# A gated mix of linear and local attention on one core: evacuations first, later weight sums, zeros between weight chunks, and KV products on 128x32 tiles

## The chip, the cores and the metric

The kernel runs on one core of a Trainium2 chip. The metric is the device time of one execution in microseconds (us). Before the change three runs took 472.9, 471.93 and 472.41 us; the median is 472.41 us. The engines are named as in the profile: PE is TensorE's matmul, PEld its weight load, DVE is VectorE, ACT is ScalarE, POOL is GpSimd, and SP is the engine whose queue issues nearly all the DMAs (SPq in the profile).

## The reference

Two attention blocks read the same input x (2048 rows of 1024), each with weights of its own, and a gate mixes their outputs:

```python
x = A_x
g = sigmoid((x * gate_w).sum(-1, keepdims=True))
return g * a + (1 - g) * b
```

Block A is linear attention with 32 heads of 32 columns, without a causal mask:

```python
phi = lambda t: jnp.where(t > 0, t + 1, jnp.exp(t)) + 1e-6
pq, pk = phi(q), phi(k)
kv = jnp.einsum("bhsd,bhse->bhde", pk, v)
z = jnp.einsum("bhsd->bhd", pk)
num = jnp.einsum("bhqd,bhde->bhqe", pq, kv)
den = jnp.einsum("bhqd,bhd->bhq", pq, z)[..., None] + 1e-6
a = (num / den) merged over heads @ wo
```

So for each head the kernel needs one 32x32 matrix kv and one column z, both sums over all 2048 rows. Block B is a softmax over the 8 positions s, s-2, ... s-14 of each row, for 32 heads, followed by its own output product `@ wo`. All inputs are bf16.

## The kernel before

**Products.** Most projections are done as block products of two by two halves with seven multiplications in place of eight (m1 to m7, `class Group`, line 235 on). They need sums of halves of the operands, built on VectorE: of x (`xsums`), of the weights (`Weights.sums`, lines 133 to 136, four operations for a whole weight matrix), and of the attention outputs (`out_sums`, line 762). Each product ends in a PSUM tile X or Y of one bank, of which there are four in all; ScalarE copies X out (line 259) or VectorE adds X or Y to a saved part (line 232).

**Stages, in the order of time.** First `vb_plain` (line 459) computes the B values of four row tiles with ordinary products, while the weights arrive in chunks of two of the eight k blocks (`vb_load`). In its loop over kc the first tile has to wait for each chunk. Before it, TensorE multiplies zeros (line 810) that come from `KVacc`, which is cleared for it. The B values then go to DRAM (`vb_store`), and the loads of later x tiles stand behind these stores on SP's queue. From about 70 to 310 us follow in turn the B keys and queries by columns (`k_group`, `q_group`), the A keys and values by rows (`ka_group`, `va_group`), and beside them the side work. From about 300 us on come the A queries (`qa_plain`, line 597), from about 360 us on the output products (`out_group`).

**Side work.** `attn` (lines 632 to 682), the KV products (`kv` inside `va_group`) and the A outputs (`qa_out`) are generators. `add_side(delay, ...)` puts them into a queue, and `side` takes a step of one of them between the products of the main loop, at a rate and not before its delay, counted in products, is over. So the delay places the TensorE work of a step. All of them write into one and the same PSUM tile of four banks (`side_ps`, `ps_s` has a single buffer). A step can start only when the step before has been read out of it:

- scores `s` (line 647) are read by the exponential on ScalarE (line 652), which makes PT;
- `o` (lines 664 and 670) is read by Ln on ScalarE (line 675) and by the copy `nB` on VectorE (line 676);
- `kps` (line 529), the KV products of one pair of row tiles, is read by the addition to `KVacc` on VectorE (line 537; a copy at line 535 the first time). After the last of eight, line 539 masks KVacc into `KVz`, which the A outputs use;
- `oA` (line 568) is read by a copy on ScalarE (line 570). Then GpSimd computes line 573 and line 574, VectorE the reciprocal (line 576), and GpSimd two products (line 579); the result is stored to `OA_d` (line 581), and comes back transposed as `oT` (line 754) for the output products.

The KV products take 128 columns of phi(k) at a time, which are four heads, against the values of these four heads with a column of ones each (4 x 33 = 132 columns). Of the 4 x 4 head blocks of each result only the four on the diagonal are used; the mask `bd` clears the others.

**Order.** TensorE and SP follow the order in which the program calls them. For the other engines a scheduler places instructions by priority and expected readiness when the kernel is built; each of these engines then works through its list in order. `defer(products, ops, gap)` hands VectorE the sums of a weight matrix, one operation every `gap` products, after `products` products: the sums of A's output weights begin 15 products after the pair-7 keys, those of B's 7 products after `plain(1, 0)`.

**In qa_plain** each row half has two PSUM tiles Q (line 610). ScalarE takes the exponential of each (line 615); when both are there, VectorE does line 618 and twice line 620, which releases the two tiles.

Of the kernel before, what the change touches and what calls it, by code (L numbers as in the profile page):

```python
# [8 lines left out]
ACT = mybir.ActivationFunctionType  # L9
ALU = mybir.AluOpType  # L10
AX = mybir.AxisListType
BF16 = mybir.dt.bfloat16
FP16 = mybir.dt.float16
F32 = mybir.dt.float32
P = 128
QB = 57
NPAIR = 9
TW = 6 * QB
# [10 lines left out]
def kernel(  # L29
# [11 lines left out]
    nc = tc.nc  # L41
# [6 lines left out]
    SCALE = float(Dh) ** -0.5  # L48
# [9 lines left out]
    consts = ctx.enter_context(tc.tile_pool(name="consts", bufs=1))  # L58
# [109 lines left out]
        return Weights(P, W, T)  # L168


    KVacc = consts.tile([P, 8, 132], F32, name="KVacc")
    nc.vector.memset(KVacc[:, 0:1, :], 0.0)
    warm = KVacc.bitcast(BF16)[:, 0, 0:256]
    W = wp.tile([P, 8, D], BF16, name="W", tag="W")
    T = tp.tile([P, 3, 4, 512], FP16, name="T", tag="T")
    T3v = kqp.tile([P, 4, 512], FP16, name="T3v", tag="kq")
# [138 lines left out]
    def add_side(delay, gen, key, kind, front=False):  # L315

        entry = [state["now"] + delay, gen, key, next(gen)[1], kind]
        if front:
            queue.insert(0, entry)
        else:  # L320
            queue.append(entry)
# [39 lines left out]
    def defer(products, ops, gap=1):  # L361


        deferred.append([state["now"] + products, list(ops), gap])
# [50 lines left out]
    gps_tile = side_ps("gps")  # L415
# [9 lines left out]
    def gate_end():  # L425
# [2 lines left out]
        nc.vector.tensor_scalar(out=omg[:], in0=omg[:], scalar1=1.0, scalar2=None, op0=ALU.add)  # L428
        nc.vector.reciprocal(out=omg[:], in_=omg[:])


    def v_tiles(name):
        if name == "va":
# [26 lines left out]
    def vb_plain(*pairs):  # L460


        vs = {pair: v_tiles("va") for pair in pairs}
        tiles = [(pair, i) for pair in pairs for i in range(2)]

        def ps_of(pair, i):
            return ps_pj.tile([P, 512], F32, name="K", tag="XY"[i] + str(pair % 2))

        def mm(ps, pair, i, j, kc):
            p, c = divmod(pair, 4)  # L470
            nc.tensor.matmul(ps[:], lhsT=xT[p][:, kc, i, c * P:c * P + P],
                             rhs=wvB.W[:, kc, 512 * j:512 * j + 512], start=kc == 0, stop=kc == 7,
                             skip_group_check=True)
        for pair, i in tiles:
            ps = ps_of(pair, i)
            for kc in range(8):
                mm(ps, pair, i, 0, kc)
            gate(tile_of(pair, i))
            v_final(vs[pair], True)(i, 0, ps[:], None)
        tiles = tiles[2:] + tiles[:2]  # L480
        ps = {t: ps_of(*t) for t in tiles}
        for k in range(4):
            for t in tiles:
                for kc in (2 * k, 2 * k + 1):
                    mm(ps[t], *t, 1, kc)
                if k == 3:
                    pair, i = t
                    v_final(vs[pair], True)(i, 1, ps[t][:], None)
                    vb_store(vs[pair], pair, i)
# [27 lines left out]
    def va_group(w, pair):  # L517
        vs = v_tiles("vA")

        def kv():  # L520
            first = kv_state["n"] == 0
            kv_state["n"] += 1
            last = kv_state["n"] == 8
            yield 0, 3
            kps = side_ps("kps")
            for i in range(2):
                pk = pks[tile_of(pair, i)]
                for c in range(8):
                    nc.tensor.matmul(kps[:, c // 2, c % 2 * 132:c % 2 * 132 + 132], lhsT=pk[:, c * P:(c + 1) * P],  # L529
                                     rhs=vs[i][:, 4 * c:4 * c + 4, :].rearrange("p h e -> p (h e)"),  # L530
                                     start=i == 0 and c % 2 == 0, stop=i == 1, skip_group_check=True)
            src = kps[:, :, 0:264]
            dst = KVacc[:].rearrange("p (a c) e -> p a (c e)", a=4)
            if first:
                nc.vector.tensor_copy(out=dst, in_=src)
            else:
                nc.vector.tensor_tensor(out=dst, in0=src, in1=dst, op=ALU.add)
            if last:
                nc.vector.tensor_tensor(out=KVz[:].rearrange("p c (g e) -> p c g e", g=4),
                                        in0=KVacc[:].rearrange("p c (g e) -> p c g e", g=4),  # L540
                                        in1=bd[:, None, :, :].broadcast_to([P, 8, 4, 33]), op=ALU.mult)
            yield 2, 2

        def done(i):
            if i == 1:
                add_side(2, kv(), 2, "kv", True)
        return Group(row_ops(w, pair), v_final(vs), done)


# [84 lines left out]
    def attn(nn, p, kT, qT, vw):  # L634

        def scores(t):
            s = side_ps("s")
            for ch in range(2):  # L640
                for j in range(3):
                    e = (3 * ch + j) * QB
                    for b in range(2):
                        q0 = q_of(t, j, b)
                        k0 = max(0, q0 - 7)
                        for g in range(4):
                            nc.tensor.matmul(s[64 * b:64 * b + 64, g, e:e + QB],  # L647
                                             lhsT=kT[32 * g:32 * g + 32, 1024 * ch + k0:1024 * ch + k0 + 64],
                                             rhs=qT[32 * g:32 * g + 32, 1024 * ch + q0:1024 * ch + q0 + QB],
                                             start=True, stop=True)  # L650
            PT = ptp.tile([P, 4, TW], BF16, name="PT", tag="PT")
            nc.scalar.activation(out=PT[:], in_=s[:, :, 0:TW], func=ACT.Exp, scale=SCALE)  # L652
            m = maskp[:, 0 if t else 1, :, :].rearrange("p i q -> p (i q)")
            nc.vector.tensor_tensor(out=PT[:], in0=PT[:], in1=m[:, None, :].broadcast_to([P, 4, TW]), op=ALU.mult)  # L654
            return PT

        def pv(t, PT):
            o = side_ps("o")
            for e in range(6):
                ch, j = divmod(e, 3)  # L660
                for g in range(4):
                    for b in range(2):
                        rows = slice(64 * b, 64 * b + 64)
                        nc.tensor.matmul(o[32 * g:32 * g + 32, 2 * b, QB * e:QB * e + QB],
                                         lhsT=vw[rows, 3 * t + j, 4 * ch + g, :],
                                         rhs=PT[rows, g, QB * e:QB * e + QB], start=True, stop=True)
            for g in range(4):
                for b in range(2):
                    rows = slice(64 * b, 64 * b + 64)
                    nc.tensor.matmul(o[32 * g:32 * g + 32, 2 * b + 1, 0:TW], lhsT=ones[rows, :], rhs=PT[rows, g, :],  # L670
                                     start=True, stop=True)
            nB = ofp.tile([P, 2, TW], F32, name="nB", tag="nB", bufs=1)
            rB = ofp.tile([P, 2, TW], F32, name="rB", tag="rB", bufs=1)
            oB = ofp.tile([P, 6, 2, QB], BF16, name="oB", tag="oB", bufs=2)
            nc.scalar.activation(out=rB[:], in_=o[:, 1:4:2, 0:TW], func=ACT.Ln)  # L675
            nc.vector.tensor_copy(out=nB[:], in_=o[:, 0:4:2, 0:TW])  # L676
            nc.scalar.activation(out=rB[:], in_=rB[:], func=ACT.Exp, scale=-1.0)
            num, r = (ap.rearrange("p b (e q) -> p e b q", e=6) for ap in (nB[:], rB[:]))
            nc.vector.tensor_tensor(out=oB[:], in0=num, in1=r, op=ALU.mult)
            nc.sync.dma_start(out=OB_d[p][2 * nn:2 * nn + 2, :, TW * t:TW * t + TW].rearrange("c p q -> p c q"),  # L680
                              in_=oB[:].rearrange("p (c j) b q -> p c (j b q)", c=2))

        last = None
        yield 0, 2
        for t in range(4):
            if t < 3:
                PT = scores(t)
                yield (1, 3) if last else (3, 3)
            if last:
                pv(*last)  # L690
                yield 1, 3
            last = (t, PT)
# [29 lines left out]
    Wo = {}  # L722

    def load_wo(k, src):
        Wo[k] = row_weights(src, 0)
# [80 lines left out]
        return Group(operands, final, nk=8, scale=sc)  # L806


    for _ in range(20):
        nc.tensor.matmul(gps_tile[:, 1, 0:256], lhsT=warm[:, 0:P], rhs=warm, start=True, stop=True)  # L810

    wkB, wqB, wqA = {}, {}, {}

# [58 lines left out]
    rows = []  # L872
    for pair in range(1, 7):
        rows += [(ka[pair],), (va[pair - 1],)]
    rows += [(ka[7], lambda: load_wo("A", A_wo), lambda: defer(15, Wo["A"].sums(), 3)), (va[6],),
             (va[7], lambda: load_wo("B", B_wo))]
    cols = []
    for nn in (1, 2, 3):
# [27 lines left out]
    load_qa(2)()  # L906
    plain(0, 0, load_qa(3))
    plain(1, 0)
    defer(7, Wo["B"].sums(), 4)
    plain(2, 0)  # L910
    plain(3, 0)
    plain(0, 1, lambda: later(3, lambda: (drain(0), out_in(9, 0, 1, 2)())))
# [40 lines left out]
```

## Time and profile before

| | |
|---|---|
| three runs, median | 472.41 us (471.93 to 472.9) |
| the profiled execution | 472.19 us |
| its span, first to last instruction | 470.3 us |
| mean granted TensorE clock | 0.993 |
| matmuls of `kps` (line 529), 8 x 16 | 8.9 us busy, 220 ns each |
| addition to KVacc (line 537), 7 times | 1257 ns each |
| copy nB (line 676), 24 times | 20.8 us busy, 867 ns each |
| GpSimd's products obA (line 579) | 23.9 us busy, 1108 ns each |
| zeros at the start (line 810), 20 matmuls | 4.1 us busy, 394 ns each |

A busy time of TensorE counts each matmul from its start to its modelled end, and neighbours overlap: 16 KV matmuls of 220 ns take less than a microsecond together. So what a group of matmuls costs TensorE is best read from where the next group starts. In the lists in order of time the columns are the start, the length of the merged piece, the engine, the line, the operation with its tiles and shapes, the count, and in brackets the idle time of the engine before it with what ended it. In the list of waits they are who waited, for whom, the sum in us, the count, and the longest.

### The profile page before, as it was taken

Reading aid. Unit: us, or ns where it says so; the run is one execution under the profiler, and the core shown is the slowest. Engines: PE = TensorE matmul, PEld = TensorE weight load, DVE = VectorE, ACT = ScalarE, POOL = GpSimd, SP = SyncE. Lnnn points to the kernel's source line nnn. Section 1 sums busy time; section 2 is a strip of 40 time slices with the busy share of each in tenths; the row PEclk is TensorE's granted clock in tenths of the full one; section 3 lists DMA queues with packets and bytes.
Section 4 is the critical chain, followed back from the end, with each engine's and each line's share of the span. In section 5 each row is a group of like instructions: output and inputs, shape, how many; then the busy total and the mean of one; then the engine's idle time right before and its main releaser. Section 6 shows DMA issues by size and latency. Waiting matters only on the chain. (4 is left out here: it accounts for less than half of the span.)

```text
span 470.3 us, 11050 instructions
## 1 busy us (share of the span) xinstructions
PE 450.5 (96%) x4656; PEld 220.0 (47%) x4732; DVE 286.0 (61%) x458; ACT 230.3 (49%) x331; POOL 64.1 (14%) x145
## 2 busy tenths in 40 slices
PE   7989999999999999999999999999999999999997
PEld 3445444444444445444444444545545444444443
DVE  0436678669748677586674856597856772165311
ACT  1233337558568485584865847535564432222221
POOL 8000000000000000000000000006877631000000
PEclk8989999999999999999999999999999999999999
DMA  7999721491110602106122055436239981599111
GB/s 175 185 219 231 256 61 63 122 258 29 45 43 20 157 13 70 29 16 148 26 58 41 16 136 179 114 114 171 59 81 180 197 192 56 102 183 195 59 46 45
DMA packets 117650, 51.60 MB, mean 110 GB/s; under 512 B 77664, under 2 KB 115552, under 8 KB 117600
## 3 DMA queue, kind: packets, MB, share of 16 engines
q1 hardware_dynamic: 117504, 50.88, 46.2%
q8 instruction: 37, 0.61, 0.6%
q0 software_dynamic: 96, 0.01, 0.2%
q14 instruction: 13, 0.11, 0.1%
HBM read 25.69 MB, written 16.79 MB: 90 GB/s over the span
## 5 line engine op out<-in xcount | busy, mean ns | idle before, releaser
L610 PE MATMUL Q<-xT,WS 128*128 128x512 bf16 x246 | 57.3, 379 | 1.0 <-DVE eq L620 0.4
L250 PEld LDWEIGHTS <-xT 128*128 128x128 bf16 (+1 forms) x352 | 33.3, 98 | 39.7 <-issue 2.2
L250 PE MATMUL X<-T,SS 128*128 128x512 f16 x176 | 45.2, 379 | 0.0
L259 ACT COPY U4s<-X 128x512 f32<-128x512 f32 x38 | 22.1, 582 | 40.7 <-PE X L250 40.7
L652 ACT ACTIVATE PT<-s 128x1368 bf16<-128x1368 f32 x24 | 31.5, 1311 | 20.9 <-PE s L647 20.8
L250 PE MATMUL Y<-W,xT 128*128 128x512 bf16 (+1 forms) x137 | 38.0, 386 | 1.8 <-issue 1.1
L250 PEld LDWEIGHTS <-SS 128*128 128x128 f16 x264 | 24.6, 98 | 28.5 <-issue 1.1
L250 PEld LDWEIGHTS <-WS 128*128 128x128 bf16 (+1 forms) x256 | 24.0, 98 | 29.2 <-issue 2.0
L610 PEld LDWEIGHTS <-WS 128*128 128x128 bf16 x256 | 24.4, 98 | 27.5 <-issue 1.1
L615 ACT ACTIVATE eq<-Q 128x512 bf16<-128x512 f32 x32 | 19.1, 598 | 31.8 <-PE Q L610 30.7
L654 DVE TENSOR_TENSOR PT<-PT,maskp 128x1368 bf16<-128x1368 bf16 x24 | 20.8, 867 | 20.8 <-ACT PT L652 20.8
L250 PE MATMUL Y<-xT,WS 128*128 128x512 bf16 (+1 forms) x128 | 32.9, 380 | 0.0
L250 PE MATMUL X<-SS,TS 128*128 128x512 f16 x128 | 32.8, 379 | 0.0
L250 PEld LDWEIGHTS <-oT 128*128 128x128 bf16 (+1 forms) x192 | 18.8, 98 | 23.4 <-issue 0.6
L250 PEld LDWEIGHTS <-TS 128*128 128x128 f16 x192 | 18.0, 98 | 20.7 <-issue 1.1
L259 ACT COPY U2s<-X 128x512 f32<-128x512 f32 x38 | 22.1, 582 | 9.1 <-PE X L250 9.1
L676 DVE COPY nB<-o 128x684 f32<-128x684 f32 x24 | 20.8, 867 | 8.7 <-ACT rB L675 8.2
L259 ACT COPY M1s<-X 128x512 f32<-128x512 f32 x38 | 22.2, 583 | 7.8 <-PE X L250 7.7
L579 POOL TENSOR_TENSOR obA<-ofv,rec 128x512 bf16<-128x512 f32 x22 | 23.9, 1108 | 8.3 <-DVE rec L576 7.7
L250 PE MATMUL Y<-W,oT 128*128 128x512 bf16 (+1 forms) x96 | 22.7, 379 | 0.6 <-DVE osb L802 0.6
L250 PE MATMUL X<-W,SS 128*128 128x512 bf16 x80 | 22.8, 388 | 0.4
L250 PE MATMUL X<-T,oS 128*128 128x512 f16 x96 | 22.7, 379 | 0.0
(125 smaller groups left out, 742.2 us busy)
## 6 DMA issues: line engine op xcount, KB each, us to landing
OB_d<-oB SPq DMA_DIRECT2D x24, 171.0 KB, 3.0
V_d<-va SPq DMA_DIRECT2D x16, 256.0 KB, 2.7
WS<-in_B_wqkv_dram SPq DMA_DIRECT2D x16, 256.0 KB, 4.2
W<-in_A_wqkv_dram SPq DMA_DIRECT2D x8, 512.0 KB, 6.2
OA_d<-obA SPq DMA_DIRECT2D x16, 256.0 KB, 2.4
out_dram<-osb SPq DMA_DIRECT2D x32, 128.0 KB, 1.9
oT<-OB_d SPq DMA_DIRECT2D x12, 256.0 KB, 4.7
vw<-V_d SPq DMA_DIRECT2D x8, 288.0 KB, 4.8
```

What stands on the lines that cost most here:

```text
L250: nc.tensor.matmul(ps[:], lhsT=lhsT, rhs=rhs, start=start and kc == 0, stop=kc == self.nk - 1, skip_group_check=True)
L259: nc.scalar.copy(out=s[:], in_=ps[:])
L579: nc.gpsimd.tensor_tensor(out=ob[:, k:k + 2], in0=of[:, k:k + 2, :, 0:32], in1=rec[:, k:k + 2].broadcast_to([P, 2, 8, 32]), op=ALU.mult)
L610: nc.tensor.matmul(ps[:], lhsT=w.W[:, kc, j * P:j * P + P], rhs=xT[p][:, kc, i, :], start=kc == 0, stop=kc == 7, skip_group_check=True)
L615: nc.scalar.activation(out=es[i][:, j, :], in_=ps[:], func=ACT.Exp)
L652: nc.scalar.activation(out=PT[:], in_=s[:, :, 0:TW], func=ACT.Exp, scale=SCALE)
L654: nc.vector.tensor_tensor(out=PT[:], in0=PT[:], in1=m[:, None, :].broadcast_to([P, 4, TW]), op=ALU.mult)
L676: nc.vector.tensor_copy(out=nB[:], in_=o[:, 0:4:2, 0:TW])
```

## The change

There are four parts.

1. **Start.** The zero tile is now the whole KVacc in its new, smaller shape (264 fp32 numbers per partition, against 132 that were cleared before). 24 instead of 20 zero matmuls run first, and in the first tile of `vb_plain` three more run ahead of each of the kc = 2, 4 and 6, where the next weight chunk begins.
2. **KV products.** Each head's 32 columns of phi(k) are multiplied by its own 33 columns of values, on a tile of 128 rows by 32 columns of the array: 64 matmuls instead of 16 for a pair. The four heads of a group land in four bands of 32 partitions of the same 33 columns, all in one PSUM bank. KVacc shrinks from 1056 to 264 numbers per partition; the mask multiplies it, broadcast four times, into the same KVz.
3. **Priority.** The exponential that reads the scores, and Ln and the copy nB that read `o`, are placed by the scheduler at high priority.
4. **Delays.** The KV products come with a delay of 3 products instead of 2, and of 5 for the last pair. The sums of A's output weights are deferred by 24 products instead of 15, those of B's by 14 instead of 7.

```diff
-    KVacc = consts.tile([P, 8, 132], F32, name="KVacc")
-    nc.vector.memset(KVacc[:, 0:1, :], 0.0)
-    warm = KVacc.bitcast(BF16)[:, 0, 0:256]
+    KVacc = consts.tile([P, 8, 33], F32, name="KVacc")
+    nc.vector.memset(KVacc[:], 0.0)
+    warm = KVacc.bitcast(BF16)[:].rearrange("p a b -> p (a b)")[:, 0:256]
...
+    def warm_up(n):
+        for _ in range(n):
+            nc.tensor.matmul(gps_tile[:, 1, 0:256], lhsT=warm[:, 0:P], rhs=warm, start=True, stop=True)
+
...
             for kc in range(8):
+                if (pair, i) == tiles[0] and kc in (2, 4, 6):
+                    warm_up(3)
                 mm(ps, pair, i, 0, kc)
...
                 for c in range(8):
-                    nc.tensor.matmul(kps[:, c // 2, c % 2 * 132:c % 2 * 132 + 132], lhsT=pk[:, c * P:(c + 1) * P],
-                                     rhs=vs[i][:, 4 * c:4 * c + 4, :].rearrange("p h e -> p (h e)"),
-                                     start=i == 0 and c % 2 == 0, stop=i == 1, skip_group_check=True)
-            src = kps[:, :, 0:264]
-            dst = KVacc[:].rearrange("p (a c) e -> p a (c e)", a=4)
+                    for g in range(4):
+                        h = 4 * c + g
+                        nc.tensor.matmul(kps[32 * g:32 * g + 32, 0, 33 * c:33 * c + 33],
+                                         lhsT=pk[:, 32 * h:32 * h + 32], rhs=vs[i][:, h, :],
+                                         start=i == 0 and c == 0, stop=i == 1, skip_group_check=True)
+            acc_ = KVacc[:].rearrange("p c e -> p (c e)")
             if first:
-                nc.vector.tensor_copy(out=dst, in_=src)
+                nc.vector.tensor_copy(out=acc_, in_=kps[:, 0, 0:264])
             else:
-                nc.vector.tensor_tensor(out=dst, in0=src, in1=dst, op=ALU.add)
+                nc.vector.tensor_tensor(out=acc_, in0=kps[:, 0, 0:264], in1=acc_, op=ALU.add)
             if last:
                 nc.vector.tensor_tensor(out=KVz[:].rearrange("p c (g e) -> p c g e", g=4),
-                                        in0=KVacc[:].rearrange("p c (g e) -> p c g e", g=4),
+                                        in0=KVacc[:, :, None, :].broadcast_to([P, 8, 4, 33]),
                                         in1=bd[:, None, :, :].broadcast_to([P, 8, 4, 33]), op=ALU.mult)
...
-                add_side(2, kv(), 2, "kv", True)
+                add_side(5 if pair == 7 else 3, kv(), 2, "kv", True)
...
-            nc.scalar.activation(out=PT[:], in_=s[:, :, 0:TW], func=ACT.Exp, scale=SCALE)
+            with tc.high_priority():
+                nc.scalar.activation(out=PT[:], in_=s[:, :, 0:TW], func=ACT.Exp, scale=SCALE)
...
-            nc.scalar.activation(out=rB[:], in_=o[:, 1:4:2, 0:TW], func=ACT.Ln)
-            nc.vector.tensor_copy(out=nB[:], in_=o[:, 0:4:2, 0:TW])
+            with tc.high_priority():
+                nc.scalar.activation(out=rB[:], in_=o[:, 1:4:2, 0:TW], func=ACT.Ln)
+                nc.vector.tensor_copy(out=nB[:], in_=o[:, 0:4:2, 0:TW])
...
-    for _ in range(20):
-        nc.tensor.matmul(gps_tile[:, 1, 0:256], lhsT=warm[:, 0:P], rhs=warm, start=True, stop=True)
+    warm_up(24)
...
-    rows += [(ka[7], lambda: load_wo("A", A_wo), lambda: defer(15, Wo["A"].sums(), 3)), (va[6],),
+    rows += [(ka[7], lambda: load_wo("A", A_wo), lambda: defer(24, Wo["A"].sums(), 3)), (va[6],),
...
-    defer(7, Wo["B"].sums(), 4)
+    defer(14, Wo["B"].sums(), 4)
```

## Prediction, made before the changed kernel was run

> **What bounds the kernel now.** I read the page first (engine shares and slices), then the list of waits with TensorE as the one that waits, then the order of time of TensorE, VectorE and GpSimd around each of its stalls, and last the compiled instruction order of both kernels, engine by engine.
>
> ```profile
> PE 450.5 (96%) x4656; PEld 220.0 (47%) x4732; DVE 286.0 (61%) x458; ACT 230.3 (49%) x331; POOL 64.1 (14%) x145
> PE   7989999999999999999999999999999999999997
> PEclk8989999999999999999999999999999999999999
> ...
> PE s L647 <- DVE nB L676: 3.2, 7, 1.0
> PE K L471 <- DMA W<-in_B_wqkv_dram: 2.2, 1, 2.2
> ```
>
> TensorE is busy from end to end, so time is won only where it stands still, where its clock is halved, or where its work shrinks. The change touches four places.
>
> Place 1, the start (order of time of TensorE; then the table of windows, whose last four fields are POOL busy, clock, DMA share, GB/s):
>
> ```profile
> 1.04 4.06 PE L810 MATMUL gps<-KVacc 128*128 128x256 bf16 x20 [1.04 <-DVE KVacc L172]
> 7.30 3.41 PE L471 MATMUL K<-W,xT 128*128 128x512 bf16 x8 [2.19 <-DMA W<-in_B_wqkv_dram]
> ...
> 8.00:11.40 3.40, 3.40 (x16) 1.37 (x16) 0.00 (x0) 0.59 (x1) 2.86 (x15) 0.50 1.10 199
> 31.90:35.30 3.40, 3.40 (x10) 1.18 (x8) 0.80 (x2) 0.59 (x1) 0.00 (x0) 0.50 1.18 198
> ```
>
> After the zeros TensorE stands for 2.19 us, and then runs at half clock for one stretch of 3.4 us. A second such stretch follows the waits for xT at 29 to 31 us.
>
> Place 2, the attention stretch, 70 to 300 us (VectorE, then TensorE):
>
> ```profile
> 173.02 0.42 DVE L498 TENSOR_SCALAR tA<-tA 128x1024 bf16<-128x1024 bf16 x1
> 173.35 0.42 DVE L499 TENSOR_SCALAR eA<-eA 128x1024 bf16<-128x1024 bf16 x1
> 173.69 0.86 DVE L676 COPY nB<-o 128x684 f32<-128x684 f32 x1
> ...
> 174.60 0.56 PE L647 MATMUL s<-qT,kT 32*64 32x57 bf16 x48 [0.48 <-DVE nB L676]
> ```
>
> The next scores need the one side tile of PSUM (four banks) that nB still reads.
>
> Place 3, the last KV products (TensorE, then VectorE):
>
> ```profile
> 309.41 1.24 PE L529 MATMUL kps<-vA,eA 128*128 128x132 bf16 x16 [1.03 <-DVE nB L676]
> ...
> 307.36 1.22 DVE L133 TENSOR_TENSOR T<-W 128x2048 f16<-128x2048 bf16 x1
> 308.49 0.86 DVE L676 COPY nB<-o 128x684 f32<-128x684 f32 x1
> ```
>
> A Wo sum of 1.2 us sits ahead of nB, and the KV products wait for nB.
>
> Place 4, the plain q groups, 317 to 360 us (GpSimd, VectorE, TensorE):
>
> ```profile
> 339.58 1.17 POOL L573 TENSOR_SCALAR rec<-of 128x32 f32<-128x32 f32 x1
> 343.73 0.32 POOL L573 TENSOR_SCALAR rec<-ofv 128x32 f32<-128x32 f32 x1
> 350.28 0.32 POOL L573 TENSOR_SCALAR rec<-of 128x32 f32<-128x32 f32 x1
> ...
> 350.95 0.35 DVE L576 RECIPROCAL rec<-rec 128x32 f32<-128x32 f32 x1 [2.89 <-POOL rec L574]
> ...
> 352.36 2.75 PE L610 MATMUL Q<-xT,WS 128*128 128x512 bf16 x12 [0.35 <-DVE eq L620]
> ```
>
> GpSimd's units of L573, L574, L579 follow each other without a hole from 327 to 353 us: 3.3 us a unit, 4.2 us where a Wo sum on VectorE lies over it (L573 takes 1.17 instead of 0.32). Its ninth unit releases the reciprocal, behind which L618 and L620 stand in VectorE's queue, and TensorE waits for L620. So here GpSimd already sets the pace.
>
> [...] the trace shows the drain (about 0.09 us before each scores block, 0.13 after it)[...].
>
> **Part by part**, against the profiled execution (472.19 us with 470.3 of span, 0.22 under the median 472.41).
>
> A. KV products. Now 16 matmuls and 0.94 us a time (127.68 to 128.62), eight times. After: 64 pairs of load and matmul on 128x32 tiles, 33 columns. No row has this tile. The nearest, L664 (48 pairs on 64x32), runs a pair in 8.3 ns in its steady part, with some 0.1 us of stalled start inside; each row group then takes a load every 16.6 ns. At 8.3 ns: 64 x 8.3 = 0.53, plus drain 0.09, inner stall 0.09, tail 0.12, in all 0.83 us, a gain of 8 x 0.11 = 0.9. If a load that fills all rows goes only at the 16.6 ns of a row group: 1.06 + 0.30 = 1.36, a loss of 8 x 0.42 = 3.3. I take -0.9, since L647 and L664 show loads into neighbouring tiles overlapping; both ends are kept. [...] The products come one product later (five for pair 7); GpSimd's memset of the next vA waits for them, but is needed 15 us later.
>
> B. Priority. ScalarE's order is the same in both kernels. VectorE's differs at three of the third scores blocks (113, 173 and 233 us): nB passes one L499, 0.34 us. At 173 and 233 TensorE gains that, 0.68 in all: Ln ends at 173.21, so nB can start at 173.36. At 113 VectorE is full from 107 to 122 us, and vA at 119.27 would stop TensorE by as much more: 0. The other waits of about 0.35 us stay, since nB there follows Ln at once. L499 and L500 finish up to 0.9 us later; their KV product is over 10 us off. B = -0.7.
>
> C. Place 3. L133 now follows the third L620 pair, so nB runs at 307.4; the KV products come 12 Q matmuls later (2.6 us) and wait for nothing. That takes away the stall and its ragged start, about 1.3 us. New on the path: 20 Q matmuls (4.3 us) between KV products and oA[...]. C = -1.3.
>
> D. The Wo sums, eight VectorE operations of 1.2 us and no DMA. Before, of eight units ahead of the ninth, four are stretched (units 3 to 6), since A's sums were over at 319.8. After, by the compiled order, A's second to fourth sums fall on units 1 to 3 and B's four on units 5 to 8: seven are stretched. GpSimd then starts unit 1 at 319.2 - 1.3 = 317.9 and needs 7 x 4.2 + 3.3 plus 0.3 for a late first = 33.0 us, so unit 9 starts at 350.9 instead of 350.3. TensorE stops there as before, now until about 353.0 instead of 352.36: C's gain goes back, with 0.7 on top. D = +2.0. Bounds: 0 if the stretches hide in gaps, +2.5. The tiles that L620 frees are ready 0.1 to 1 us ahead of use until then. SP's order is unchanged; oT's loads stand behind the eighth OA_d store and move with it.
>
> E. Start. 4 + 9 zero matmuls. The four run in the wait of 2.19 us; so does the longer memset (0.17 us before for half the elements). The nine lie between chunks that landed at 7.26, 7.95, 8.61 and 9.36 us. At full clock they cost 9 x 0.11 = 1.0, hidden in these waits, and tile 1 starts when its xT lands, 10.2 instead of 10.77, and at full clock: -0.85 by the end of this block. The V_d stores and xT loads behind it follow, so the gain survives the waits at 29 to 31. If the clock still halves, they cost 0.21 each on the path: +0.8. Between 4.6 and 8.0 TensorE is on record for 1.1 of 3.4 us now, for some 1.7 after; between 28.5 and 31.9 it was on record for 1.78, partly one-column gate products, and the clock still halved. [...] so I take -0.4, between the ends but nearer the gain.
>
> Sum: -0.9 - 0.7 - 1.3 + 2.0 - 0.4 = -1.3, so 472.19 - 1.3 = 470.9 us.
>
> **Rivals.** (1) GpSimd doesn't give it back (D = 0): -3.3, 468.9 us. For: C is a plain stall; against: the unbroken GpSimd chain. (2) The clock halves at the start in spite of the zeros: E = +0.8, 472.1, no change. For: 1.7 us on record is no more than the 1.78 that did not save the later stretch; against: a third of that was gate products. (3) Slower: loads into 128x32 tiles take turns. Place: the eight KV blocks; price 16.6 ns a pair, A = +3.3, so 475.1 us. It decides from 13.2 ns a pair on (1.14 us a block, where the sum passes +1.16). For: all row groups are in use at once[...]; against: L664's 8.3 ns.
>
> **How the numbers follow.** Forecast 0.42, rival 1 0.27, rival 2 0.17, rival 3 0.12, anything else on the slow side 0.02. About 0.2% (0.94 us) is what a measurement tells from no change: faster is under 471.47, slower over 473.35. Faster: four fifths of the forecast, rival 1, a little of rival 2: 0.62. Same: the rest of the forecast and most of rival 2: 0.22. Slower 0.16. The range runs from rival 1 with a better start, 468.4, to rival 2 with a kps block of 1.1 us, 473.2; rival 3 is mostly left out.
>
> **What would show it.** kps blocks of about 0.83 us (A); nB right after L498 at two places with 0.34 us less wait (B); no TensorE wait at the last kps (C); L573 at 1.17 in seven units instead of four and a longer stop at the Q after the ninth (D); PEclk full in the third 3.4 us (E). Wrong would be a kps block over 1.14 us, or a stop at the ninth unit no longer than before.

## The result, and the profile after

The changed kernel takes 469.03 us, median of 4 executions (468.55 to 470.43); the kernel before takes 472.17 in the same comparison. The ratio is 0.9936, with a 95% interval of 0.9912 to 0.996. The profiled execution took 468.55 us (span 466.7), against 472.19 (470.3) before.

Under this lies something that one profile of each kernel can't show: TensorE's granted clock at the start differs from execution to execution of the same kernel. In the experiments below the kernel before ran 107 times with its mean clock listed. In 58 of them it was 0.991 to 0.993 (median 472.27 us), in 24 between, and in 25 it was 0.999 or 1.0 (median 470.44). The profile of before, at 0.993, is of the common kind; the profile of the changed kernel, at 1.0, is the only one of its four executions with that clock. So part of the 3.1 us isn't work saved.

The listed mean has a limit: it counts from the first clock record of an execution on, and the tables show 1.00 where nothing is on record. In the trace of the due times alone, below, the records begin at 13.40 us and the mean is 0.995, though the first eight products took 3.57 us, as in the half-clock stretch of before (3.41; at full clock the eight at 14.92 us of before take 1.89). So one mean can stand for different starts. At 0.999 or 1.0 the kernel before took 469.4 to 470.6 us in fifteen executions and 471.3 to 471.7 in ten; at 0.995 or 0.996 it took 469.9 to 470.7 in ten and 473.0 to 474.3 in fourteen. What parts the two lots isn't shown, as only one execution of the kernel before was traced.

The page of the changed kernel, busy time of the engines and the clock granted in 40 slices:

```profile
PE 453.2 (97%) x5129; PEld 217.3 (47%) x5129; DVE 281.0 (60%) x458; ACT 230.1 (49%) x331; POOL 65.7 (14%) x145
...
PEclk9999999999999999999999999999999999999999
```

The busy time of TensorE isn't to be compared with the 450.5 us of before, where 76 matmuls are missing from the records (4656 against 4732 loads). The clock has no slice under 9 any more, from its first record at 6.66 us on; ahead of it the 24 zeros took 0.22 us each, twice the 0.11 of the nine later ones. The list of waits, with TensorE waiting:

```profile
PE s L654 <- DVE nB L685: 1.9, 5, 0.7
...
PE Q L617 <- DVE eq L627: 1.7, 1, 1.7
...
PE Y L250 <- DVE osb L811: 1.0, 1, 1.0
PE K L475 <- DMA W<-in_B_wqkv_dram: 0.9, 1, 0.9
...
PE Q L617 <- DVE vA L232: 0.5, 1, 0.5
```

The waits for nB fell from 3.2 us to 1.9, that for the first weight chunk from 2.2 to 0.9, and that at the last KV products is gone. New are 1.7 us for eq (0.35 before), 1.0 for osb at 432 us, and 0.5 for vA. The start in the table of windows, first the 3.41 us from the first clock record on, then the two half-clock stretches of before (the clock is third from the end):

```profile
6.66:10.07 3.41, 2.73 (x18) 1.67 (x18) 0.00 (x0) 0.00 (x0) 2.87 (x15) 1.00 1.21 264
8.00:11.40 3.40, 3.40 (x28) 2.01 (x26) 0.00 (x0) 0.59 (x1) 2.86 (x15) 1.00 1.13 197
31.90:35.30 3.40, 3.40 (x17) 1.57 (x16) 1.70 (x4) 1.75 (x3) 0.00 (x0) 1.00 1.44 164
```

Both stretches that ran at 0.50 ran at 1.00. TensorE in order of time, at the places that the prediction speaks of:

```profile
1.19 5.30 PE L433 MATMUL gps<-KVacc 128*128 128x256 bf16 x24 [1.19 <-DVE KVacc L172]
7.34 0.59 PE L475 MATMUL K<-W,xT 128*128 128x512 bf16 x2 [0.86 <-DMA W<-in_B_wqkv_dram]
...
126.44 0.68 PE L537 MATMUL kps<-vA,eA 128*32 128x33 bf16 x64
127.05 1.04 PE L250 MATMUL X<-W,xT 128*128 128x512 bf16 x4
...
304.46 2.75 PE L617 MATMUL Q<-xT,WS 128*128 128x512 bf16 x12 [0.49 <-DVE vA L232]
307.14 0.68 PE L537 MATMUL kps<-vA,eA 128*32 128x33 bf16 x64
...
348.35 2.75 PE L617 MATMUL Q<-xT,WS 128*128 128x512 bf16 x12 [1.66 <-DVE eq L627]
...
432.06 1.89 PE L250 MATMUL Y<-W,oT 128*128 128x512 f16 x8 [1.02 <-DVE osb L811]
```

A kps block lasts 0.61 us from its start to the next product's (126.44 to 127.05), where it was 0.94. It begins 0.31 us after the product ahead of it (126.13), where before it was 0.22 (127.46 to 127.68): about 0.1 us is added there now. The last one at 307.14 waits for nothing. VectorE, at the place where nB stood behind L499 before (that line is L505 now):

```profile
170.38 0.42 DVE L504 TENSOR_SCALAR tA<-tA 128x1024 bf16<-128x1024 bf16 x1
170.72 0.86 DVE L685 COPY nB<-o 128x684 f32<-128x684 f32 x1
171.50 0.42 DVE L505 TENSOR_SCALAR eA<-eA 128x1024 bf16<-128x1024 bf16 x1
```

And GpSimd's first unit, one stretched unit, and the ninth:

```profile
313.90 0.34 POOL L580 TENSOR_SCALAR rec<-ofv 128x32 f32<-128x32 f32 x1 [26.05 <-ACT ofv L577]
314.33 1.09 POOL L581 TENSOR_TENSOR rec<-rec,nel 128x32 f32<-128x32 f32 x1
...
342.17 1.17 POOL L580 TENSOR_SCALAR rec<-ofv 128x32 f32<-128x32 f32 x1
...
346.27 0.32 POOL L580 TENSOR_SCALAR rec<-of 128x32 f32<-128x32 f32 x1
```

Laying the starts of TensorE's scores, kps and oA blocks of the two traces side by side gives an account of the 3.6 us of span:

| where (us in the trace of before) | after minus before, running | step |
|---|---|---|
| scores at 70 us | -2.19 | clock of the start |
| scores at 114.8, then 134.8 | -2.53, then -2.41 | -0.34 (nB), given back at 119; first kps block -0.22 |
| scores at 293 | -4.19 | two nB waits, -0.68 in all, and five more kps blocks at -0.22 |
| first oA at 317 | -5.32 | seventh kps block -0.22; the eighth and its wait -0.91 |
| oA after the ninth unit, 355 | -4.01 | stop at the ninth unit, +1.31 |
| 366 to 380 | -4.76 | two waits of before, 0.58 and 0.17, absent |
| Y at 432 in the trace after | -3.58 | new wait for osb, +1.18 |

### The profile page after: what moved, and what is told of

Read it like the earlier page. It is cut to its first block, busy times and chain, and to the rows that moved or that the text cites. A ratio compares the mean times of both kernels' runs of the same rounds, so it can differ in the third digit from the quotient of the medians.

```text
span 466.7 us, 11921 instructions
## 1 busy us (share of the span) xinstructions
PE 453.2 (97%) x5129; PEld 217.3 (47%) x5129; DVE 281.0 (60%) x458; ACT 230.1 (49%) x331; POOL 65.7 (14%) x145
## 5 line engine op out<-in xcount | busy, mean ns | idle before, releaser
L617 PE MATMUL Q<-xT,WS 128*128 128x512 bf16 x256 | 59.0, 379 | 2.2 <-DVE eq L627 1.7
L250 PE MATMUL Y<-W,xT 128*128 128x512 bf16 (+1 forms) x152 | 39.1, 380 | 0.6 <-DVE vA L232 0.6
```

The source lines that it names most:

```text
L250: nc.tensor.matmul(ps[:], lhsT=lhsT, rhs=rhs, start=start and kc == 0, stop=kc == self.nk - 1, skip_group_check=True)
L617: nc.tensor.matmul(ps[:], lhsT=w.W[:, kc, j * P:j * P + P], rhs=xT[p][:, kc, i, :], start=kc == 0, stop=kc == 7, skip_group_check=True)
```

## The experiments

Each was timed beside the kernel before on its chip (472.27 us in the first group, 471.76 in the second, 471.85 in the third, 472.22 in the last). The first four make one part of the change alone on the kernel before.

**The start alone**

```diff
-    for _ in range(20):
+    warm_up(24)
...
+                if (pair, i) == tiles[0] and kc in (2, 4, 6):
+                    warm_up(3)
```

> The kernel before with the start part alone (24 zero matmuls ahead of the first weight chunk instead of 20, and three each between its four chunks). Theory: the zeros raise the clock's grant before the first chunk's work, so both stretches of 3.4 us at half clock (8.0 to 11.4 and 31.9 to 35.3 us) go: full clock from about 6.7 us on, 2.0 to 2.2 us less on TensorE by 40 us, and all of it kept to the end, about -2.1 us of time. Rival (the prediction's step E): only the first stretch goes and the second stays, since it follows the waits for xT: -0.4 to -0.8 us. Second rival: [...] the zeros don't help in another execution: within 0.5 us of before, with the first stretch still at half clock.

469.64 us, ratio 0.9952 (0.9933 to 0.997). Five of six executions had a clock of 0.999 or 1.0. In the trace TensorE is 2.01 us earlier at 70 us and keeps that. The first theory held on this chip. By its median the start alone buys 2.6 us of the 3.1 of the whole change; but the changed kernel, with as many zeros, had the full clock in one of four executions and not in five of six.

**The KV products alone**

```diff
-                    nc.tensor.matmul(kps[:, c // 2, c % 2 * 132:c % 2 * 132 + 132], ...
+                    for g in range(4):
+                        h = 4 * c + g
+                        nc.tensor.matmul(kps[32 * g:32 * g + 32, 0, 33 * c:33 * c + 33], ...
```

(and KVacc in its new shape, with its copy, addition and mask, as in the change)

> The kernel before with the KV products alone on 128x32 tiles (and KVacc of 8 x 33 columns), due two products later as before. Theory: a block of 64 pairs lasts 0.61 us instead of 0.94 and the stretch around it is shorter by 0.22 us, eight times: -1.7 us. Rival (the prediction's step A): 0.83 us a block, -0.9 us. Second rival: the gain at the last block is lost to the wait for nB, which stays here since the due times are those of before: seven blocks count, -1.5 us.

468.07 us, ratio 0.9913 (0.9893 to 0.9932): more than any theory said. The excess is the clock: all four executions were at 1.0, and the trace is 2.15 us ahead before the first kps block. From there to the first oA it gains 1.67 us more, which is the part's own worth.

```profile
154.97 0.68 PE L531 MATMUL kps<-vA,eA 128*32 128x33 bf16 x64
155.58 0.60 PE L250 MATMUL X<-SS,TS 128*128 128x512 f16 x2
...
305.75 0.38 PE L531 MATMUL kps<-vA,eA 128*32 128x33 bf16 x32 [1.03 <-DVE nB L677]
306.35 0.38 PE L531 MATMUL kps<-vA,eA 128*32 128x33 bf16 x32 [0.22 <-DVE vA L232]
```

The block takes 0.61 us, and the last one still waits for nB and vA, as its due time is the old one; 0.16 us of its gain of 0.22 remains. Why this kernel, with 20 zeros, ran at full clock four times of four is open: its memset is longer and its zeros start 0.14 us later, which was not tried by itself.

**The due times alone**

```diff
-                add_side(2, kv(), 2, "kv", True)
+                add_side(5 if pair == 7 else 3, kv(), 2, "kv", True)
...
-defer(15, Wo["A"].sums(), 3)
+defer(24, Wo["A"].sums(), 3)
...
-    defer(7, Wo["B"].sums(), 4)
+    defer(14, Wo["B"].sums(), 4)
```

> The kernel before with the due times alone changed (Wo A sums 24 products later instead of 15, Wo B sums 14 instead of 7, KV products 3 and for the last pair 5 instead of 2). Theory (the prediction's steps C and D): the wait at the last KV products goes (about -1.0 us there), seven of GpSimd's units on L573/L574 are stretched instead of four, and TensorE's stop at the Q after the ninth unit grows from 0.35 to about 1.5 to 2 us: the gain is given back, time within -0.5 to +0.7 us of before. Rival (the prediction's first rival): GpSimd doesn't give it back, -1.3 us.

473.11 us, ratio 1.0018 (1.0004 to 1.0031): slower, by 0.84 us a little beyond the theory's upper end. Its trace starts 1.40 us behind that of before, as its clock rose late (13.40 us), so the steps are counted from there: the last KV products gain 0.69 us by the first oA, and the stop at the ninth unit takes 1.31 back:

```profile
354.42 2.75 PE L610 MATMUL Q<-xT,WS 128*128 128x512 bf16 x12 [1.66 <-DVE eq L620]
```

Seven units are stretched, and the net is +0.62. The rival, that GpSimd doesn't give it back, falls.

**The priority alone**

```diff
+            with tc.high_priority():
-            nc.scalar.activation(out=rB[:], in_=o[:, 1:4:2, 0:TW], func=ACT.Ln)
-            nc.vector.tensor_copy(out=nB[:], in_=o[:, 0:4:2, 0:TW])
+                nc.scalar.activation(out=rB[:], in_=o[:, 1:4:2, 0:TW], func=ACT.Ln)
+                nc.vector.tensor_copy(out=nB[:], in_=o[:, 0:4:2, 0:TW])
```

(and the same around the Exp of the scores)

> The kernel before with the priority of Exp, Ln and nB alone. Theory (step B): nB passes one L499 at two places that count (173 and 233 us), 0.34 us each, so -0.7 us; the one at 113 us is given back at 119. Rival: priority matters at every scores block, so the waits on nB (3.2 us in all) fall to near nothing: -2 us or more. Second rival: the two waits saved come back where vA or eA is late: within 0.2 us of before.

472.06 us, ratio 0.9989 (0.997 to 1.0007): no difference. The second rival's outcome, but at a place that no theory named. The trace gains 0.34 us at 173 and again at 233, then loses more at the last KV products, whose due time is the old one:

```profile
307.59 0.86 DVE L678 COPY nB<-o 128x684 f32<-128x684 f32 x1
308.37 1.22 DVE L133 TENSOR_TENSOR T<-W 128x2048 f16<-128x2048 bf16 x1
309.50 0.86 DVE L681 TENSOR_TENSOR oB<-nB,rB 128x684 bf16<-128x684 f32 x1
310.28 0.69 DVE L232 TENSOR_TENSOR vA<-Y,U2s 128x512 bf16<-128x512 f32 x1
```

nB now goes first, and vA, which the second half of the KV products needs, comes fourth: TensorE waits 1.87 us for it at 311.02, and the block ends with the trace 0.77 us worse than at 293. So the priority pays only together with the later due times.

The next four start from the changed kernel.

**Without the nine zeros between the chunks**

```diff
-                if (pair, i) == tiles[0] and kc in (2, 4, 6):
-                    warm_up(3)
```

> The changed kernel without the nine zero matmuls between the first weight chunks (the 24 ahead of them and the longer memset stay). Theory: [...] the executions keep a mean clock of 0.996 to 1.0, and the time is within 0.3 us of the changed kernel at the same clock. Rival (the prediction's step E): the nine keep the clock up in the window in which the chunks land; without them most executions show 0.992 to 0.993 as the kernel before does, both half-clock stretches come back, and the time is 1.5 to 2.2 us longer than the changed kernel's 469.0.

468.2 us, ratio 0.9939 (0.9917 to 0.9961), and seven of eleven executions at 1.0. The nine zeros aren't what keeps the clock. At 1.0 the times fall into two lots, 467.3 to 467.4 (three) and 468.0 to 468.5 (four).

**GpSimd's two small operations as one on VectorE**

```diff
-            nc.gpsimd.tensor_scalar(out=rec[:, :, :, 0], in0=of[:, :, :, 32], scalar1=EPS, ...
-            nc.gpsimd.tensor_tensor(out=rec[:, :, :, 0], in0=rec[:, :, :, 0], in1=nel..., op=ALU.mult)
+            nc.vector.scalar_tensor_tensor(out=rec[:, :, :, 0], in0=of[:, :, :, 32], scalar=EPS,
+                                           in1=nel..., op0=ALU.add, op1=ALU.mult)
```

> The changed kernel with L580 and L581 (GpSimd's sum and product of 128x32 ahead of the reciprocal) as one operation of VectorE. Theory (step D): GpSimd's chain of units sets the stop of 1.66 us at the Q after the ninth unit; with 0.9 to 1.8 us less for each unit it isn't the pace any more, the stop goes to 0.3 us or less, and the time falls by 1.3 to 1.7 us at the same clock. Rival: the stop is set by VectorE (ScalarE's copy of oA, the Wo sums of 1.75 us and L625, L627 in its queue); then it stays over 1 us and the time moves by less than 0.3 us.

466.27 us, ratio 0.9893 (0.9865 to 0.992); at a clock of 0.999 or 1.0, 465.63 to 466.71. TensorE runs through the place of the stop:

```profile
344.96 0.62 PE L575 MATMUL oA<-KVz,eq 128*128 128x132 bf16 x8
345.42 3.62 PE L617 MATMUL Q<-xT,WS 128*128 128x512 bf16 x16
348.87 0.62 PE L575 MATMUL oA<-KVz,eq 128*128 128x132 bf16 x8
```

By the second of these oA blocks it is 1.82 us further ahead of the changed kernel than at the first. GpSimd's chain is the cause of the stop; the rival, VectorE, falls, though VectorE got the work (0.20 us where the two GpSimd operations took 0.56).

**A fifth buffer in the ring of osb**

```diff
-name="ering", bufs=4
+name="ering", bufs=5
```

> The changed kernel with five buffers instead of four in the ring that holds osb (and the e and eq tiles). Theory: the new wait of 1.02 us at 432 us is osb waiting for a buffer whose store stands in SP's queue behind the transposes of oT; with a fifth buffer osb is written as soon as its product is done, the wait goes, and the end comes 1.0 to 1.2 us earlier at the same clock. Rival: osb waits for something else (the sums of oT ahead of it in VectorE's queue, ScalarE's M1s), or SP's queue still holds the ring: the wait stays, within 0.3 us of the changed kernel.

467.43 us, ratio 0.9925 (0.9896 to 0.9953). The wait at 432 is gone, but it is gone as well in the trace of the kernel without the nine zeros, which has four buffers. So by itself that shows little. VectorE's osb for the same product tells more. In the changed kernel:

```profile
431.25 0.75 DVE L811 SCALAR_TENSOR_TENSOR osb<-Y,omg,M1s 128x512 bf16<-128x512 f32 x1 [4.15 <-PE Y L250]
```

in the kernel without the nine zeros:

```profile
428.43 0.75 DVE L809 SCALAR_TENSOR_TENSOR osb<-Y,omg,M1s 128x512 bf16<-128x512 f32 x1 [3.04 <-DMA out_dram<-osb]
```

and with five buffers:

```profile
425.95 0.75 DVE L811 SCALAR_TENSOR_TENSOR osb<-Y,omg,M1s 128x512 bf16<-128x512 f32 x1 [0.57 <-issue]
```

The product itself ends near 425.9 in all three. With four buffers osb waits for the store of an older osb, and in the changed kernel 2.8 us longer than in the other: long enough there to stop TensorE. The reader should not trust the releaser named first: PE Y was done 5 us before. SP's queue shows why the store is late, in the changed kernel:

```profile
423.80 4.37 SPq L763 DMA_TRANSPOSE oT<-OA_d  x2
428.26 7.29 SPq L814 DMA_DIRECT2D out_dram<-osb  x7
```

Seven stores stand behind the transposes. In the kernel without the nine zeros the same stores begin at 424.64 us and with five buffers at 425.61, so in both traces SP's queue was also earlier. The pair of transposes before these took 5.89 us in the changed kernel, 4.35 and 4.63 in the other two; why, is open. No trace shows five buffers beside a queue as late as 428.26. At a clock of 0.999 or 1.0 the two kernels with five buffers (this one, and the one with 34 zeros below) took 467.3 to 467.5 and 465.6 to 466.0, one lot each in nine executions; with four there were two lots, 0.7 to 1 us apart, in this kernel's two neighbours above. That supports the ring as the cause of the upper lot but doesn't prove it: a different start under the same mean clock stays a rival.

**The Wo sums back at their old due times**

```diff
-defer(24, Wo["A"].sums(), 3)
+defer(15, Wo["A"].sums(), 3)
...
-    defer(14, Wo["B"].sums(), 4)
+    defer(7, Wo["B"].sums(), 4)
```

> The changed kernel with the Wo sums at their due times of before (15 and 7 products), the KV products at 3 and 5 as in the change. Theory (step D): four GpSimd units are stretched instead of seven, the stop at the ninth unit falls from 1.66 to 0.3 to 0.6 us, while the KV products' later due time alone keeps them clear of nB: 1.0 to 1.4 us faster than the changed kernel at the same clock. Rival (the reason for which the sums would have to be moved): a Wo sum of 1.2 us is ahead of nB again near 307 us, and vA, nB and with them the KV products are late by as much: the gain is lost there, within 0.4 us of the changed kernel.

469.97 us, ratio 0.9963 (0.9946 to 0.998). Both theories have half of it. The stop at the ninth unit falls from 1.66 to 0.37 us, as step D says. But a Wo sum is ahead of vA again (VectorE):

```profile
304.45 0.86 DVE L685 COPY nB<-o 128x684 f32<-128x684 f32 x1
305.23 1.22 DVE L133 TENSOR_TENSOR T<-W 128x2048 f16<-128x2048 bf16 x1
306.36 0.87 DVE L688 TENSOR_TENSOR oB<-nB,rB 128x684 bf16<-128x684 f32 x1
307.14 0.69 DVE L232 TENSOR_TENSOR vA<-Y,U2s 128x512 bf16<-128x512 f32 x1
```

and TensorE pays twice, first for the wait and then in the clock (order of time, then the windows on both sides of the clock's fall):

```profile
307.88 4.44 PE L617 MATMUL Q<-xT,WS 128*128 128x512 bf16 x12 [2.41 <-DVE vA L232]
```

```profile
304.74:308.15 3.41, 1.00 (x6) 0.36 (x5) 3.41 (x5) 0.60 (x1) 0.00 (x0) 1.00 0.00 1
308.15:311.56 3.41, 3.41 (x10) 1.18 (x9) 0.81 (x1) 0.29 (x1) 0.00 (x0) 0.50 0.92 243
```

Twelve matmuls take 4.44 us instead of 2.75. In this execution the place costs 3.6 us against the changed kernel (1.51 behind at 289 us, 5.11 at the first oA), the ninth unit gives 1.28 back. At a clock of 0.999 or 1.0 the six executions took 467.56 to 468.28, no more than the changed kernel; the other sixteen, at a lower clock, make the median.

**Both remedies together**

The two edits above, the VectorE operation and the fifth buffer, in one kernel.

> The changed kernel with both: L580 and L581 as one VectorE operation, and five buffers in the ring of osb. Theory: the two waits are separate places (1.66 us at the ninth unit, about 1.0 to 1.2 us at 432 us where it occurs), so the gains add: an execution at a mean clock of 0.999 or more takes 465.6 to 465.9 us, each time, and none shows 466.7 as one of the kernel with four buffers did. Rival: the wait at 432 us is chance of the transposes and not of the ring; then some executions at full clock still show about 466.7.

467.61 us, ratio 0.9921 (0.9898 to 0.9944). The expectation can't be read from the times, since none of six executions was at full clock: all have 0.994 to 0.996. The trace does show that the gains add. It is 1.54 us behind the changed kernel at 70 us, and its span is 1.25 shorter: 2.79 us gained, where 2.7 to 2.9 were expected. Its start, and the windows from its first clock record on:

```profile
1.20 4.11 PE L433 MATMUL gps<-KVacc 128*128 128x256 bf16 x24 [1.20 <-DVE KVacc L172]
7.68 1.01 PE L475 MATMUL K<-W,xT 128*128 128x512 bf16 x2 [2.37 <-DMA W<-in_B_wqkv_dram]
...
3.93:7.34 3.41, 1.38 (x13) 1.07 (x11) 0.00 (x0) 0.00 (x0) 3.13 (x20) 1.00 0.79 218
7.34:10.75 3.41, 3.07 (x11) 1.55 (x11) 0.00 (x0) 0.00 (x0) 2.81 (x15) 0.50 1.28 231
```

Here the zeros took 4.11 us, not 5.30: the clock rose while they ran, at 3.93 us, so they ended sooner and left a hole of 2.37 us, and the chunks' products then ran at half clock. With the same 24 zeros the hole was 0.86 us in the profile of the changed kernel, where the clock rose at 6.66, after them.

**The same with 34 zeros ahead of the first chunk**

```diff
-    warm_up(24)
+    warm_up(34)
```

> The same with 34 zero matmuls ahead of the first weight chunk instead of 24, so that they last to about the chunk's landing at 7.3 us even at half clock. Theory: [...] with no hole of 1.1 to 2.0 us there nearly all executions show a mean clock of 0.999 to 1.0, against about half of them with 24, and the median falls by up to 0.5 us or, where the other kernel's executions are at full clock too, by nothing. Rival: [...] the executions with 0.992 to 0.996 are as frequent as with 24. Second rival: the extra zeros delay the first chunk's products: 0.2 to 0.8 us longer.

465.88 us (465.6 to 467.5), ratio 0.9888 (0.9861 to 0.9915), five of six at 1.0. This is the best version found: against the kernel before it saves 1.1%, where the changed kernel saves 0.6%.

```profile
1.20 6.52 PE L433 MATMUL gps<-KVacc 128*128 128x256 bf16 x34 [1.20 <-DVE KVacc L172]
7.72 0.59 PE L475 MATMUL K<-W,xT 128*128 128x512 bf16 x2
```

The hole is closed. The first chunk's product begins 0.04 us later than in the trace above with 24 zeros (7.68), and no wait for a weight chunk is left in the list.

**The changed kernel without the priority**

The three operations of the priority edit stand outside of it again.

> The changed kernel without the priority of Exp, Ln and nB. Theory (step B): nB stands behind one L499 (now L505) again at 173 and 233 us, 0.34 us each, and at 113 us it is given back: +0.7 us at the same clock. Rival: as alone on the kernel before, where the time hardly moved: the priority is worth nothing in the changed kernel too, within 0.2 us at the same clock.

469.12 us, ratio 0.9943 (0.9923 to 0.9963); at a clock of 0.999 or 1.0, 467.59 to 468.56, which by time alone can't be told from the neighbouring kernels. The trace can tell: behind the changed kernel it is 1.98 us at 112, 1.65 at 126 (given back), 1.97 at 172 and 2.31 at 230, a step of 0.32 to 0.34 at each of the two places that count, and nB stands behind L505:

```profile
172.36 0.42 DVE L505 TENSOR_SCALAR eA<-eA 128x1024 bf16<-128x1024 bf16 x1
172.69 0.86 DVE L683 COPY nB<-o 128x684 f32<-128x684 f32 x1
```

**The kernel before with 34 zeros, and nothing else**

```diff
-    for _ in range(20):
+    for _ in range(34):
```

> The kernel before with 34 zero matmuls ahead of the first weight chunk instead of 20, and nothing else. Theory: most of the changed kernel's 3.1 us is the granted clock of the first 40 us; with no hole before the first chunk nearly all executions show 0.999 or more, and the median falls by 0.8 to 2.2 us to the 469.4 to 471.6 us that the executions of before with that clock took. Then the change's own part, at equal clock, is 1.4 to 2.5 us. Rival: the stretch after the waits for xT at 29 to 31 us halves the clock in any case: mean clock 0.996 in most, 0 to 0.8 us less.

469.42 us (468.74 to 471.05), ratio 0.9951 (0.9937 to 0.9964); 17 of 22 executions at 0.999 or 1.0, against 4 of the 27 of before beside it. One number in one line buys nearly what the whole change does. The seventeen took 468.74 to 469.71 us, the four 469.77 to 470.39, so the listed mean isn't all that the zeros change. Its trace is 2.48 us ahead at 70 us, about as far as the changed kernel was at that place (2.19):

```profile
1.05 6.28 PE L810 MATMUL gps<-KVacc 128*128 128x256 bf16 x34 [1.05 <-DVE KVacc L172]
7.31 0.59 PE L471 MATMUL K<-W,xT 128*128 128x512 bf16 x2
```

## Why the prediction came out as it did

The forecast was 470.9 us and -1.3; measured are 469.03 and -3.1. The sign and the range hold, and the forecast is 1.9 us too slow. In the two profiles the difference is 3.6 us of span: -2.19 from the start (E, put at -0.4), -1.82 from A to D (put at -0.9), -0.75 from two waits that went and +1.18 from a new one. By its steps:

**A, KV products: right mechanism, mis-sized.** -0.9 was taken, from 8.3 ns a pair and 0.30 us of drain, inner stall and tail. What the prediction calls the drain is read from the scores blocks of before: a block begins 0.31 us after the full-tile product ahead of it (134.44 to 134.75), where full-tile products follow each other at 0.22. Measured for kps are 0.61 us and 0.1 ahead of the block, 0.71 instead of 0.83, and -1.67 for the eight (the part alone). The inner stall of some 0.1 us, which the nearest row has, doesn't occur here: from the first start to the last are 0.50 us, 8.0 ns a pair, with no gap over 0.03, and the tail of 0.11 is as predicted. The slower rival, loads that take turns at 16.6 ns, is excluded. The addition to KVacc takes 422 ns, where it took 1257.

**B, priority: right in the changed kernel.** -0.7 was predicted, at 173 and 233 us, with 113 given back at 119. The account shows -0.34, -0.34, and the give-back; taking the priority away again shows the same two steps. What the prediction didn't say is that this needs step C's due times: alone, the priority lost it all to vA at the last KV products.

**C and D, the due times: each too large, their sum right.** C was -1.3 and D +2.0, together +0.7; alone on the kernel before they gave -0.69 and +1.31, together +0.62. C missed that the wait doesn't vanish: vA stands behind nB, and the Q products wait 0.49 us for the PSUM tile that it frees. D had 33.0 us from the first to the ninth unit; measured 32.4 (313.90 to 346.27), as 7 x 4.16 + 3.31, without the 0.3 us for a late first unit. The mechanism is as predicted, with seven units stretched and a longer stop, and taking the load off GpSimd removes the stop. That the sum of C and D came out right is luck: their errors, 0.6 and 0.7 us, cancel.

**E, the start: this is the term that failed.** It was put at -0.4, the author's estimate between two ends, and only for the first half-clock stretch; the second, at 32 us, was left in place. In the pair of profiles E is -2.19: 0.67 by the end of the first stretch, of which 0.51 is left after the waits for xT, and 1.68 because the second stretch is gone. This compares a common execution of before with the best one of the changed kernel. The runs show that it is a matter of shares: a mean clock of 0.999 or 1.0 in 25 of 107 executions with 20 zeros in the kernel before, in 25 of 60 over all kernels with 24 and nine, in 22 of 28 with 34. (Executions of one kernel tend to fall alike, so these are not independent draws.)

The traces show what goes with the fall of the clock. In all but that of the due times alone the clock's records begin somewhere from 3.93 to 6.68 us. In five of these thirteen TensorE was on record for 1.12 to 1.45 us of the first 3.41, and the next 3.41 ran at half clock; in eight it was 1.78 to 3.41, and the clock stayed. With 24 zeros the three that fell have their first record at 3.93 to 4.38 us, and the zeros, sped up early, left holes of 1.96 to 2.37 us; the five that held have it at 5.40 to 6.68, with holes of 0.86 to 1.58. So with 24 zeros an earlier first record goes with a larger hole, and the larger hole with half clock; what sets the time of the first record isn't shown. With 34 zeros there was no hole; the records of both of their traces begin at 5.97 us or later, though, so none shows them with an early one.

The rival of a clock that halves in spite of the zeros was mis-sized as well. Three of the changed kernel's four executions show 0.996, and the three fallen traces with 24 zeros are at 70 us still 0.54 to 0.70 us ahead of before, where the rival had +0.8: the second stretch is absent in them. It is absent in all eight traces with 24 zeros, and why isn't shown. In the 3.41 us ahead of it TensorE was on record for 1.79 us before; in the changed kernel it was 1.77 in the window from 27.14 us on, and no fall followed.

**Not foreseen:** the wait of 1.18 us for osb at 432, and the waits of 0.58 and 0.17 us at 366 and 379 that went. The last two went in the kernel before with 34 zeros as well, so they aren't the change's doing.

The trace of the kernel before with 34 zeros and that of the changed kernel without the nine zeros are both at a clock of 1.0: 468.97 and 467.32 us. At equal clock, then, parts A to D bring 1.65 us where osb doesn't wait at 432, and 0.42 (468.97 to 468.55) in the profile where it does (the traces' starts are within 0.3 us of each other at 70 us). The prediction's A to D made -0.9, half of what their places gained, nearly all of the rest in A; the larger error, 1.8 us, is the clock's.

## What to carry to other kernels

Before comparing two profiles, compare the granted clock of many executions of each, and where its records begin: here a half-clock stretch of 3.4 us cost up to some 1.75 us (465.75 and 467.5 in one kernel, 469.25 and 471.0 in another), about as much as the best single edit. Let zeros that are to hold the clock last until the first data lands, also when the clock rises while they run: 34 did so in both their traces, and 22 of 28 executions had a mean clock of 0.999 or 1.0; 24 did so in none, and it was 32 of 71 (25 of 60 with the nine between the chunks, seven of eleven without). When an operation is moved out of a queue, follow the chain that then sets the pace: here GpSimd took back 1.31 us where the later sums had gained 0.69, and moving 0.56 us of small work a unit off it was worth 1.82.

## What the hardware showed that was not expected

- Tiles of 128x32 with 33 columns: 64 pairs of load and matmul in 0.61 us with the tail (8.0 ns a pair from start to start), after about 0.1 us that is added ahead of the block. A load takes 93 ns on record in these blocks; one of the full tiles of before took 98.
- The clock falls in the middle of the kernel too: with the Wo sums back, one wait of 2.41 us, in 3.41 us in which TensorE was on record for 1.00, was followed by 3.41 us at half clock. After the stop of 1.66 us in the changed kernel and the wait of 1.87 us with the priority alone the clock stayed.
- VectorE's and GpSimd's operations take longer over each other, both ways. L580 takes 1.17 us under a Wo sum instead of 0.32. A Wo sum takes 1.75 us where it starts under a product of GpSimd (at 317.32 us, the product ends at 317.98), and 1.22 where only L581 lies under it (at 314.10).
